# Sliding-window attention, then a gated feed-forward block, on one core: score units of 128 queries shifted by 64 in 64x64 tiles

## The chip, the core and the metric

The kernel runs on one core of one Trainium2 chip. The metric is the device time of one execution in microseconds (us). The kernel before took 308.55 us (median of three runs, 308.38 to 308.95). The profiled execution is one more run of the same kernel, and it took 309.3 us; its trace spans 307.5 us from the first instruction to the last, and 1.8 us lie around the span.

## What is computed

There are 8 batches, 8 heads, 576 tokens and 64 elements a head. A query sees itself and the 127 keys before it, with a bias that falls linearly with distance, by another slope in each head. The attention output is put together to rows of 512 and goes through two matrix products with a gate between them.

```python
B, H, S, D = q.shape                                   # 8, 8, 576, 64
scores = scale * np.matmul(q, k.transpose(0, 1, 3, 2))
rel = pos[:, None] - pos[None, :]
mask = (rel >= 0) & (rel < 128)
scores = np.where(mask, scores - slopes[h] * rel, -1e9)
attn = softmax(scores)                                 # over keys
x = concat_heads(attn @ v)                             # 4608 x 512
h = x @ w_in                                           # 512 x 2048
out = (h * np.cos(h)) @ w_out                          # 2048 x 512, written as f32
```

## The kernel before

**Products of the block.** The 4608 tokens are nine chunks of 512. For a chunk, `moe1` (L758) makes 16 groups of four matmuls (L764, 512 columns each) from the transposed rows `xT`; ScalarE takes the cosine as a sine (L769) and VectorE multiplies (L773) into `gT`. `moe2` (L806) makes 64 matmuls a chunk (L817), whose results ScalarE or VectorE copies out (L824, L825) and a store on the SyncE queue writes to memory (L829). The two halves of a chunk are 128 matmuls of 512 columns.

**Attention units.** `units` (L547) cuts a batch into eight units. The first holds queries 0 to 127 for all heads with 128 key columns a head; six hold 128 queries of four heads with 256 key columns (the block before and the own block); the last holds the last 64 queries for all heads. A unit is 1024 score columns over 128 key partitions. `scores` (L554) makes it with pairs of 64x128 matmuls, one head of a pair in array rows 0 to 63 and the other in 64 to 127 (L573), into two banks of PSUM: `SLOT` gives banks 4 and 5, 6 and 7, 2 and 3 to the units of a visit. `exps` (L596) makes one exponential of 1024 columns (L600); `mask` (L605) multiplies by the exponential of the bias, which is 0 outside the window (L619); `pv` (L622) multiplies by the values, 65 columns a matmul with a column of ones for the sum (L635, L639, L647, L649), 128 wide stationary blocks of the probabilities; `norm` (L662) divides (L672, L675, L684, L686). The rows are then transposed into `xT`: `x_pe` (L693) on TensorE with a copy behind it (L726, L735), or `x_dma` (L740) with a transposing DMA on the SyncE queue (L748, L751).

**Order.** `attention(us, phase)` (L835) takes the units of one phase, of which each chunk has one up to chunk 6 (`QUOTA` units, L342), and makes them in visits of the sizes in `GROUPS` (L338): one call of `scores` for all units of a visit, the exponentials, then for each unit mask, values, norm and transpose. The first four units of a phase go to `xT` by DMA (list `begin`). Then come the loads for later batches: `load_v` on the GpSimd queue, which waits for the DMAs in `begin`, `dma_transposes` (L412) of q and k on the SyncE queue, and `load_nat` (L403) on GpSimd, which waits until those transposes have read the buffer.

All of this only registers operations with a planner (`Plan`, L35). `Plan.schedule` (L95) gives each operation a start from written costs (`occ`, `lat`), takes the lowest priority number first (values 1, scores 2, `moe1` 5, `moe2` 6), and allows one ScalarE function table at a time (phase c exponentials have table 2c+2, the sines of chunk c have table 2c+1). The order on each engine is then fixed: at run time an engine waits for the semaphores of its next instruction and passes over nothing. So `moe2` of chunk c fills TensorE while phase c runs, and `moe1` of chunk c+1 follows.

Of the kernel before, what the change touches and what calls it, by code (L numbers as in the profile page):

```python
# [13 lines left out]
NBLK = 5  # L14
# [273 lines left out]
def bass_alibi_sliding__then__act_gcu_kernel(  # L288
# [8 lines left out]
    with ExitStack() as ctx:  # L297
        def sb(name, shape, dt=BF16):
            return ctx.enter_context(nc.sbuf_tensor(name, shape, dt))
# [17 lines left out]
        NP = 6  # L317
        p_all = sb("p", [128, NP, 1088])
        P = [p_all[:, i, :] for i in range(NP)]
# [13 lines left out]
        off = sb("off", [128, 2, 128], F32)  # L333

        ps = ctx.enter_context(nc.psum_tensor("ps", [128, 8, 512], F32))
# [57 lines left out]
        def load_v(b, order=range(NBLK), behind=()):  # L393
            for t in order:
# [6 lines left out]
                   occ=900, lat=7 * rows)  # L401

        def load_nat(which, src, b):  # L403
            fns = []
            for t in range(NBLK):
                rows = 128 if t < 4 else 64
                fns.append(lambda e, t=t, rows=rows: e.dma_start(  # L407
                    nat[which][0:rows, t, :, :],
                    src[b, :, 128 * t:128 * t + rows, :].rearrange("h p d -> p h d")))
            op("pool", fns, w=[("nat", which)], dma=f"ldn{which}", occ=4400, lat=5500)  # L410
# [29 lines left out]
        def constants():  # L440
# [15 lines left out]
            for i in range(2):  # L456
                op("dve", lambda e, i=i: e.memset(vp[i][:, :, :, 64:65], 1.0), w=[("vinit", i)],
                   pri=5 * i)
                op("dve", lambda e, i=i: e.memset(vp[i][64:128, 4, :, 0:64], 0.0),
                   w=[("vinit", i)], occ=270, pri=5 * i)  # L460
# [7 lines left out]

        def tail_zero(b):
            op("dve", lambda e: e.memset(  # L470
                tr["k"][b % 2][:, :].rearrange("p (c k t) -> p c k t", c=NBLK, k=NPAIR)[
                    :, 4, :, 64:128], 0.0), w=[("tr", "k", b % 2), ("ktail", b % 2)], occ=250,
               lat=300)

# [70 lines left out]


        def units(b):  # L547
            return [(b, 0, 0)] + [(b, qb, hh) for qb in range(1, 4) for hh in range(2)] + [
                (b, 4, 0)]

        def t_first(u):
            return S * u[0] + 128 * u[1]

        def scores(us, slot, after=()):  # L554

            def f(e):
                ins = None
                for n, u in enumerate(us, slot):
                    b, qb, hh = u
                    banks = [SLOT[n], SLOT[n] + 1]  # L560
                    acc = u in BIASED
# [15 lines left out]
            for n, u in enumerate(us, slot):  # L577
                keys += tkeys(u)
                held += [("B", SLOT[n] + x) for x in range(2)]
                occ += 250 if u[1] == 4 else 230  # L580
                if u in BIASED:
                    b, qb, hh = u
                    for x in range(2):
# [6 lines left out]
                           occ=216, lat=379, pri=2, after=after)  # L590
            return op("pe", f, r=keys, w=held, occ=occ, lat=occ + 165, mode=1, pri=2)

        pcount = [0]
        pbuf = {}
# [10 lines left out]
        def mask(u):  # L605
            b, qb, hh = u
            i = pbuf[u]
            if u in BIASED:
                return
            if qb == 0:  # L610
                p = P[i][:, 0:1024].rearrange("p (x k f) -> p x k f", x=2, k=4)
# [4 lines left out]
            else:  # L616
# [3 lines left out]
               r=[("P", i), ("EM", 0), ("EM", 1)], w=[("P", i)], occ=600, lat=690, pri=1)  # L620

        def pv(us):  # L622

            def f(e):
                ins = None
                for u, ub in us:
                    b, qb, hh = u
                    i, V = pbuf[u], vp[b % 2]
                    if qb in (0, 4):
                        for x in range(2):  # L630
# [22 lines left out]
            for u, ub in us:  # L653
                b, qb, hh = u
                wide = qb in (0, 4)
                reads += [("P", pbuf[u]), ("vinit", b % 2)]
                reads += [("v", b % 2, t) for t in range(max(0, qb - 1), qb + 1)]
                held += [("B", x) for x in ([ub, ub + 1] if wide else [ub])]
                occ += 480 if qb == 4 else 240
            op("pe", f, r=reads, w=held, pri=1, occ=occ, lat=occ + 165)  # L660

        def norm(u, ub, n):  # L662
            b, qb, hh = u
            rc = rec[n % 4]
            if qb in (0, 4):
                m = 64 if qb else 128
# [20 lines left out]
                o, U[:, :, :, 0:64], rv[:, :, :, None].broadcast_to([128, 2, 2, 64]), ALU.mult),  # L687
               r=[("rec", n % 4)], w=[("B", ub), key], occ=340, lat=425, pri=0)

        def xkeys(prs, t0, n):  # L690
            return [("xT", pr, t // 64) for pr in prs for t in range(t0, t0 + n, 64)]

        def x_pe(u, ub, n):  # L693
            b, qb, hh = u
            t0 = t_first(u)
            every = range(NPAIR)
            if qb in (0, 4):
                m = 64 if qb else 128
# [40 lines left out]

        def x_dma(u, n):  # L740

            b, qb, hh = u
            t0 = t_first(u)
            if qb in (0, 4):
                m = 64 if qb else 128
                src_, key = (xtl[b % 2], ("xtl", b % 2)) if qb else (xfirst, "xfirst")
                return op(
                    "sp", [lambda e: e.dma_start_transpose(xT[:, :, t0:t0 + m], src_[:, :])],  # L748
                    r=[key], w=xkeys(range(NPAIR), t0, m), dma=f"xt{b % 2}" if qb else "xf",
                    occ=1250, lat=500)  # L750
# [84 lines left out]
        def attention(us, phase):  # L835

            begin, made, g = [], [], 0
            sizes = ([[3, 2, 2]] + GROUPS + [[], []])[phase + 1]
            own = phase >= 0 and 3 in sizes
            for many in sizes:  # L840
# [13 lines left out]
                else:  # L854
                    scores(some, 0)
                    for n, u in enumerate(some):
                        exps(u, n, 2 * phase + 2)
                if not own:
# [6 lines left out]
                else:  # L865
                    sets = [[x] for x in zip(some, SLOT)]
                for set_ in sets:
# [4 lines left out]
                    for u, ub in set_:  # L872
# [4 lines left out]
                        after.append((soon, t_first(u) // CH > phase + 1, u, ub, n))  # L877
                    for soon, late, u, ub, n in after:
                        if soon:
                            begin.append(x_dma(u, n))  # L880
# [37 lines left out]
        for c in range(NCH):  # L918
            if c == 0:
# [63 lines left out]
```

## Time and profile before

| what | value |
|---|---|
| median of three runs | 308.55 us |
| profiled execution | 309.3 us |
| span of its trace | 307.5 us |
| TensorE busy | 302.1 us, 98% |
| ScalarE busy | 199.9 us, 65% |
| VectorE busy | 194.4 us, 63% |
| GpSimd busy | 95.7 us, 31% |
| mean granted TensorE clock | 1.000 |

A row of the instruction groups reads: line, engine, operation, what it writes and reads, shape, count, then busy us and mean ns of one, then the idle time of the engine just before them and what ended it. PE is TensorE, PEld its weight loads, ACT ScalarE, DVE VectorE, POOL GpSimd, SP SyncE; a q behind the name is the engine's queue of DMA issues. A row of the chain of work reads: start in us, length in us, engine, what is written, line and count.

### The profile page before, as it was taken

Reading aid. Unit: us, or ns where it says so; the run is one execution under the profiler, and the core shown is the slowest. Engines: PE = TensorE matmul, PEld = TensorE weight load, DVE = VectorE, ACT = ScalarE, POOL = GpSimd, SP = SyncE. Lnnn points to the kernel's source line nnn. Section 1 sums busy time; section 2 is a strip of 40 time slices with the busy share of each in tenths; the row PEclk is TensorE's granted clock in tenths of the full one; section 3 lists DMA queues with packets and bytes.
Section 4 is the critical chain, followed back from the end, with each engine's and each line's share of the span. In section 5 each row is a group of like instructions: output and inputs, shape, how many; then the busy total and the mean of one; then the engine's idle time right before and its main releaser. Section 6 shows DMA issues by size and latency. Waiting matters only on the chain.

```text
span 307.5 us, 6459 instructions
## 1 busy us (share of the span) xinstructions
PE 302.1 (98%) x2605; PEld 156.5 (51%) x2605; DVE 194.4 (63%) x402; ACT 199.9 (65%) x267; POOL 95.7 (31%) x120
## 2 busy tenths in 40 slices
PE   7899999999999999999999999999999999999996
PEld 5585455445544555445544554455445554444444
DVE  6587667586578566856785568657966588742000
ACT  6897765885487746883688378736964588752211
POOL 8996200555055505550348033900400000000000
PEclk9999999999999999999999999999999999999999
DMA  7999999999699939999699959994991420001112
GB/s 161 179 206 206 207 158 174 167 152 166 125 123 142 175 104 141 131 162 109 157 130 160 151 98 158 153 182 98 154 118 44 113 70 0 0 0 70 68 73 97
DMA packets 149788, 39.08 MB, mean 127 GB/s; under 512 B 138624, under 2 KB 144768, under 8 KB 149760
## 3 DMA queue, kind: packets, MB, share of 16 engines
q0 software_dynamic: 100144, 18.10, 80.1%
q1 hardware_dynamic: 49344, 20.33, 32.8%
q8 instruction: 20, 0.33, 0.4%
q10 hardware_dynamic: 272, 0.26, 0.3%
q14 instruction: 8, 0.07, 0.1%
HBM read 36.70 MB, written 9.44 MB: 150 GB/s over the span
## 4 chain that ended last, share of the span: by engine, by line
PE 88%; DMA 9%; POOL 2%; issue 0%; ACT 0%; POOLq 0%; ACTq 0%
PE ps L817 41%; PE ps L764 36%; DMA w_outb<-in_moe_w_out_dram 7%; PE ps L573 5%; DMA krows<-in_k_dram 2%; PE ps L647 2%; PE ps L649 2%; PE ps L635 1%; PE ps L639 1%; POOL qrows L389 0%; PE ps L726 0%; PE ps L514 0%; PE ps L587 0%; POOL w_inb L428 0%; POOL w_outb L435 0%; POOL krows L389 0%
## 5 line engine op out<-in xcount | busy, mean ns | idle before, releaser
L817 PE MATMUL ps<-w_outb,gT 128*128 128x512 bf16 (+2 forms) x592 | 136.8, 374 | 0.3 <-DMA w_outb<-in_moe_w_out_dram 0.3
L764 PE MATMUL ps<-xT,w_inb 128*128 128x512 bf16 x544 | 122.7, 379 | 0.0
L773 DVE TENSOR_TENSOR gT<-ps,cos 128x512 bf16<-128x512 f32 x136 | 90.6, 688 | 21.3 <-ACT cos L769 16.3
L769 ACT ACTIVATE cos<-ps,halfpi 128x512 f32<-128x512 f32 x136 | 90.1, 688 | 19.3 <-PE ps L764 14.4
L764 PEld LDWEIGHTS ps<-xT,w_inb 128*128 128x128 bf16 x544 | 51.8, 98 | 59.8 <-DVE gT L798 0.7
L817 PEld LDWEIGHTS ps<-w_outb,gT 128*128 128x128 bf16 x592 | 53.3, 98 | 56.5 <-DMA w_outb<-in_moe_w_out_dram 1.2
L600 ACT ACTIVATE p<-ps 128x1024 bf16<-128x1024 f32 x64 | 61.4, 1024 | 31.4 <-PE ps L573 31.2
L396 POOL DMA_DIRECT2D vp<-in_v_dram x40 | 33.8, 866 | 88.2 <-DMA xT<-xnat 65.8
L619 DVE TENSOR_TENSOR p<-p,emask 128x1024 bf16<-128x1024 bf16 x58 | 39.2, 683 | 25.5 <-ACT p L600 25.5
L824 ACT ACTIVATE ob<-ps 128x512 f32<-128x512 f32 (+2 forms) x21 | 12.1, 577 | 42.2 <-PE ps L817 42.1
L407 POOL DMA_DIRECT2D qnat<-in_q_dram x30 | 25.3, 872 | 19.0 <-DMA qt<-qnat 19.0
L407 POOL DMA_DIRECT2D knat<-in_k_dram x30 | 25.3, 876 | 15.1 <-DMA kt<-knat 12.1
L825 DVE COPY ob<-ps 128x512 f32<-128x512 f32 x16 | 10.9, 683 | 16.1 <-PE ps L817 16.1
L686 DVE TENSOR_TENSOR xnat<-ps,rec 128x256 bf16<-128x256 f32 x48 | 19.9, 421 | 1.4
L573 PE MATMUL ps<-qt,kt 64*128 64x128 bf16 (+1 forms) x576 | 19.2, 211 | 0.1
L573 PEld LDWEIGHTS ps<-qt,kt 64*128 64x128 bf16 x576 | 14.5, 94 | 9.6 <-DVE xnat L686 3.4
L647 PEld LDWEIGHTS ps<-vp,p 128*128 128x128 bf16 x192 | 14.2, 97 | 9.2 <-issue 6.4
L647 PE MATMUL ps<-vp,p 128*128 128x65 bf16 x192 | 17.3, 193 | 0.4 <-ACT p L600 0.4
L649 PE MATMUL ps<-vp,p 128*128 128x65 bf16 x192 | 17.3, 193 | 0.0
L649 PEld LDWEIGHTS ps<-vp,p 128*128 128x128 bf16 x192 | 13.1, 97 | 2.3
L684 DVE RECIPROCAL rec<-ps 128x4 f32<-128x4 f32 x48 | 8.2, 176 | 5.2 <-PE ps L649 4.5
L600 ACT ACT_TABLE_LOAD x7 | 9.0, 1283 | 0.1
(63 smaller groups left out, 144.6 us busy)
## 6 DMA issues: line engine op xcount, KB each, us to landing
out_dram<-ob SPq DMA_DIRECT2D x35, 256.0 KB, 2.2
vp<-in_v_dram POOLq DMA_DIRECT2D x32, 128.0 KB, 6.9
qnat<-in_q_dram POOLq DMA_DIRECT2D x24, 128.0 KB, 6.6
knat<-in_k_dram POOLq DMA_DIRECT2D x24, 128.0 KB, 4.9
w_outb<-in_moe_w_out_dram POOLq DMA_DIRECT2D x4, 512.0 KB, 22.3
w_inb<-in_moe_w_in_dram POOLq DMA_DIRECT2D x3, 512.0 KB, 11.4
qrows<-in_q_dram POOLq DMA_DIRECT2D x1, 576.0 KB, 15.1
krows<-in_k_dram POOLq DMA_DIRECT2D x1, 576.0 KB, 18.1
```

Of the source, the lines that this page charges most:

```text
L396: op("pool", [lambda e, t=t, rows=rows: e.dma_start(vp[b % 2][0:rows, t, :, 0:64], v[b, :, 128 * t:128 * t + rows, :].rearrange("h p d -> ...
L407: fns.append(lambda e, t=t, rows=rows: e.dma_start(nat[which][0:rows, t, :, :], src[b, :, 128 * t:128 * t + rows, :].rearrange("h p d -> p ...
L573: ins = e.matmul(ps[:, banks[x], c0:c0 + n_], keys_ap(b, x, pr, kc), query_ap(b, x, pr, qb, n_), start=not acc, stop=stop)
L600: op("act", lambda e: e.activation(P[i][:, 0:1024], ps[:, banks[0]:banks[0] + 2, :].rearrange("p a b -> p (a b)"), ACTF.Exp, scale=0.125), ...
L619: op("dve", lambda e: e.tensor_tensor(p, p, m, ALU.mult), r=[("P", i), ("EM", 0), ("EM", 1)], w=[("P", i)], occ=600, lat=690, pri=1)
L647: e.matmul(o, P[i][:, c0:c0 + 128], V[:, qb - 1, h, 0:65], start=True, stop=False)
L649: ins = e.matmul(o, P[i][:, c0 + 128:c0 + 256], V[:, qb, h, 0:65], start=False, stop=True)
L686: op("dve", lambda e: e.tensor_tensor(o, U[:, :, :, 0:64], rv[:, :, :, None].broadcast_to([128, 2, 2, 64]), ALU.mult), r=[("rec", n % 4)], ...
L764: op("pe", lambda e, kc=kc: e.matmul(ps[:, bank, :], w_in[:, kc, 128 * fc:128 * fc + 128], xT[:, kc, r0:r0 + CH], start=(kc == 0), stop=(k ...
L769: op("act", lambda e: e.activation(cosb[ci][:, :], ps[:, bank, :], ACTF.Sin, bias=halfpi[:, 0:1]), r=["halfpi"], w=[("B", bank), ("cos", c ...
L773: op("dve", lambda e: e.tensor_tensor(gT[gi][:, fc, :], ps[:, bank, :], cosb[ci][:, :], ALU.mult), r=[("cos", ci)], w=[("B", bank)] + [("g ...
L817: op("pe", lambda e, t=t, fc=fc, bank=bank, j0=j0, j1=j1: e.matmul(ps[:, bank, 0:j1 - j0], gT[gi][:, fc, 128 * t:128 * t + 128], w_out[:, ...
```

## The change

Batches 0 and 1 stay as they are. For batches 2 to 7 (`banded`):

- **Units.** Eight equal units, (j, half of the heads), j from 0 to 3. Unit j holds queries 64+128j to 191+128j and needs 192 key columns a head in place of 256: both 64-key halves of block j against all 128 queries, and one 64x64 corner for each half from the neighbouring blocks. Queries 0 to 63 of a batch hang on the two units with j = 0, whose spare corner is used for them.
- **Scores.** 16 matmuls in 64x64 tiles for a unit: eight of 128 columns and eight of 64, in fours over the four tiles.
- **Visits.** `GROUPS` gives phases 2 to 5 two visits of four units in place of 3, 3 and 2. In a visit of four the units lie side by side in banks 2 to 7 (`home`), and one exponential covers 768 columns of two units; values go to banks 2, 5, 4, 7 (`SIDE`), those of queries 0 to 63 to banks 3 and 6. Phase 1 has visits of 4, 3 and 1, and the last unit of batch 1 is moved behind four units of batch 2.
- **Last phase.** The nine units of phase 6 become five in phase 6 (visits of 4 and 1) and four in a new phase 7.
- **Masks.** Two multiplications of 512 elements a unit in place of one of 1024, and a third of 256 for j = 0; the factor tables are made in `band_factors` during chunk 0 (three iotas on GpSimd, some ten VectorE operations, 24 exponentials on ScalarE).
- **Values.** Eight matmuls a unit, and four more for j = 0. Half of them need the values shifted by 64 rows: `copy_v` makes them by three DMAs from SBUF to SBUF on the GpSimd queue behind each `load_v`, which wait for its landing. `tail_zero` is gone.

```diff
-        GROUPS = [[2] * 4] + [[3, 3, 2]] * 5 + [[3] * 3]
+        GROUPS = [[2] * 4, [4, 3, 1]] + [[4, 4]] * 4 + [[4, 1], [4]]
+        SIDE, SIDE_KEY = [2, 5, 4, 7], [3, 3, 6, 6]
-        QUOTA = [8, 8, 8, 8, 8, 8, 9]
+        QUOTA = [8, 8, 8, 8, 8, 8, 5, 4]
...
+        def copy_v(b):
+            V, W = vp[b % 2], vb[b % 2]
+            op("pool", [
+                lambda e: e.dma_start(W[0:64, 0:4, :, :].rearrange("p t h c -> p (t h c)"),
+                                      V[0:64, 1:5, :, :].rearrange("p t h c -> p (t h c)")),
...
+               r=[("v", b % 2, t) for t in range(NBLK)] + [("vinit", b % 2)],
...
+               dma=f"cv{b % 2}", occ=2200, lat=3000)
...
+        def band_factors():
...
+            for h in range(H):
...
+                    op("act", lambda e, o=o, lo=lo, hi=hi, s=slopes[h]: e.activation(
+                        o, bdif[:, lo:hi], ACTF.Exp, scale=s),
+                       r=["bdif"], w=w + ["bem"], occ=180 + (hi - lo) * 5 // 7,
+                       lat=280 + (hi - lo) * 5 // 7, table=2, pri=7)
...
         def units(b):
+            if banded(b):
+                return [(b, j, hh) for j in range(4) for hh in range(2)]
...
+        def band_scores(e, u, n, side):
...
+            for i in range(2):
+                for half in range(2):
+                    for x in range(2):
...
+                        ins = e.matmul(flat[64 * half:64 * half + 64, c0:c0 + 128],
+                                       kt[lo, j, pr, 64 * half:64 * half + 64], two,
+                                       start=True, stop=True)
+            for i in range(2):
+                for half in range(2):
+                    for x in range(2):
...
+                        ins = e.matmul(flat[64 * half:64 * half + 64, c0:c0 + 64], kk, qq,
+                                       start=True, stop=True)
...
+        def exps_side(some, n, table):
...
+            for x in range(2):
+                c0 = home(n, True, x)
+                op("act", lambda e, x=x, c0=c0: e.activation(
+                    p_all[:, i:i + 2, 384 * x:384 * x + 384],
+                    flat[:, c0:c0 + 768].rearrange("p (u f) -> p u f", u=2), ACTF.Exp,
+                    scale=0.125),
...
+                op("dve", lambda e: e.tensor_tensor(p1, p1, own_em[:, gs, :], ALU.mult),
+                   r=[("P", i), "bem"], w=[("P", i)], occ=330, lat=420, pri=1)
+                op("dve", lambda e: e.tensor_tensor(
+                    o, p2[:, :, None, :].broadcast_to([128, 4, 2, 64]),
+                    out_em[0 if qb else 1][:, gs, :].rearrange("p g (y f) -> p g y f", y=2),
+                    ALU.mult), r=[("P", i), "bem"], w=[("P2", i)], occ=330, lat=420, pri=1)
...
+                            e.matmul(o, P[i][:, c0:c0 + 128], V[:, qb, h, 0:65],
+                                     start=True, stop=False)
+                            ins = e.matmul(o, P[i][:, c1:c1 + 128], W[:, qb, h, 0:65],
+                                           start=False, stop=True)
+                        for m in range(4 if qb == 0 else 0):
...
+                            ins = e.matmul(ps[:, kbank[u], 65 * m:65 * m + 65],
+                                           pk[hh][:, c0:c0 + 128], W[:, 0, 4 * hh + m, 0:65],
+                                           start=True, stop=True)
...
+        every.insert(19, every.pop(15))
...
                 load_nat("k", k, 2)
+                band_factors()
...
                 load_v(next_v, behind=begin)
+                copy_v(next_v)
...
-                if next_t < 4:
-                    tail_zero(next_t)
```

More of the change, by code (lines that the diff above doesn't have):

```diff
@@ L578, in scores @@
                 keys += tkeys(u)
[L579 to L580 removed]
+                held += [("B", x) for x in (home_banks(n, side) if banded(u[0]) else
+                                            [SLOT[n], SLOT[n] + 1]) if ("B", x) not in held]
+                occ += 185 if banded(u[0]) else 250 if u[1] == 4 else 230
                 if u in BIASED:
@@ L838, in attention @@
             sizes = ([[3, 2, 2]] + GROUPS + [[], []])[phase + 1]
-            own = phase >= 0 and 3 in sizes
+            own = phase >= 0 and max(sizes + [0]) > 2
             for many in sizes:
@@ L878, in attention @@
                     for soon, late, u, ub, n in after:
+                        if banded(u[0]) and u[1:] == (0, 1):
+                            x = x_dma(u, n, True)
+                            begin += [x] if soon else []
                         if soon:
```

189 lines of the change are left out of this document (166 added, 23 removed).

## The prediction

> **What bounds the kernel now.** I read the page first: its busy times, its slices, then the chain of work that ended last.
>
> ```profile
> PE 302.1 (98%) x2605; PEld 156.5 (51%) x2605; DVE 194.4 (63%) x402; ACT 199.9 (65%) x267; POOL 95.7 (31%) x120
> PE   7899999999999999999999999999999999999996
> PEclk9999999999999999999999999999999999999999
> DMA  7999999999699939999699959994991420001112
> PE 88%; DMA 9%; POOL 2%; issue 0%; ACT 0%; POOLq 0%; ACTq 0%
> ```
>
> PE is busy in every slice but the first two and the last, at full clock; the chain is PE's for 88% of the span, and the DMA's 9% lie in the start. A busy PE can still run below its rate, so the stretches of chunks 3 and 4 come next (us, then busy us of each engine), and the pieces of the chain inside the second.
>
> ```profile
> core 0: us, PE busy (x) PEld busy (x) DVE busy (x) ACT busy (x) POOL busy (x), PEclk, DMA share, GB/s
> 121.50:153.40 31.90, 31.90 (x271) 16.05 (x271) 22.47 (x45) 21.52 (x28) 12.00 (x15) 1.00 1.45 139
> 153.40:184.80 31.40, 31.40 (x269) 15.86 (x268) 21.34 (x43) 22.55 (x30) 12.66 (x17) 1.00 1.48 135
> ```
>
> ```profile
> 165.02 2.16 PE ps L817 x10
> 167.18 0.79 PE ps L573 x32
> 167.96 3.77 PE ps L817 x17
> ...
> 172.44 0.24 PE ps L635 x8
> ...
> 175.30 0.78 PE ps L573 x24
> 176.07 2.05 PE ps L817 x9
> ...
> 180.84 0.55 PE ps L573 x16
> ```
>
> Ten matmuls of `moe2` take 2.16, so 0.216 each. The 128 matmuls of a chunk are then 27.65. Scores are three pieces, 0.79 + 0.78 + 0.55 = 2.12. Values are 72 matmuls a batch at 0.24 / 8 = 0.03, so 2.16. That is 31.9, the whole stretch (its edges cut off a few matmuls of neighbours, either way): nothing waits, and **what is taken from PE is taken from the time**, what is taken from ACT alone is not. What PE must wait for newly is added in full, since its order is fixed.
>
> **The price of score matmuls.** x24 against x16 is eight matmuls, four pairs, for 0.23: 0.0575 a pair of 128 columns. The x16 piece is 8 pairs, 0.46, so entering a visit costs 0.09. The x32 piece holds the unit with 16 matmuls of 64 columns and two others; against x24 it is 0.01 more for 16 of 64 in place of 8 of 128, so a pair of 64 columns costs 0.24 / 8 = 0.03, and one start comes every 0.015. Leaving a visit shows in the next piece: 17 x 0.216 = 3.67 of 3.77, 9 x 0.216 = 1.94 of 2.05, about 0.10. A visit costs about 0.2 beside its matmuls.
>
> **A. Scores, 48 units.** Before: seven units of four pairs and one of eight small pairs a batch, 7 x 0.23 + 0.24 = 1.85, six times 11.1. After: 8 matmuls of 128 and 8 of 64 a unit, in fours over four tiles. No run here shows four tiles at once. The pairs of L573 share the array by rows. The transposes of L514 share it by columns (the weight loads' shapes: 64x128 against 128x64):
>
> ```profile
> 9.94 0.57 PE ps L514 x16
> L573 PEld LDWEIGHTS ps<-qt,kt 64*128 64x128 bf16 x576 | 14.5, 94 | 9.6 <-DVE xnat L686 3.4 <-issue 3.4 <-ACT xT L735 0.8
> L514 PEld LDWEIGHTS ps<-ident,qrows 128*64 128x64 bf16 x64 | 1.8, 110 | 0.5 <-issue 0.4
> ```
>
> Sixteen in 0.57, less 0.09 of entry, are 0.06 a pair of 128 columns: columns overlap as rows do. Both together should let four run in the time of two: a unit is 2 x 0.0575 + 2 x 0.03 = 0.175, 48 are 8.4, so **A = -2.7**. Bounds: four in the time that 64 columns need anywhere would be 4 x 0.03 = 0.12, 5.8 in all, -5.3, which I exclude for the 128 column halves since none in the trace passes below 0.0575; above, a start every 0.015, the tightest in the trace, is 0.24 a unit, +0.4; two at a time is 0.35 a unit, +5.7. I take 0.175, as both kinds of pairs overlap fully.
>
> The column tiles' loads are longer, 110 ns against 94; at 128 columns that is hidden, and at 64 nothing shows it. If the two small groups took a long pair's 0.0575 for it, the unit would be 0.23 and A nothing. The Trainium skill, page "TensorEngine Tiling (Array Packing)", section "Gotcha 2: Feature Incompatibilities", says that column tiling excludes the fast weight load; the longer loads agree, and by it alone A would lie between this nothing and the -2.7.
>
> **B. Visits.** Phases 2 to 5 go from three to two: four visits at 0.2, **-0.8**. Phase 1 keeps three, phases 6 and 7 have three for phase 6's three. One visit of phase 1 mixes old and new tiles: one more change, **+0.1**.
>
> **C. Values and transposes on PE.** Values are 6 x 8 + 2 x 12 = 72 matmuls a batch, as before: **0**. Transposes by `x_pe` behind phase 0 go from 8 matmuls (four units) to 12, by the rule of `soon` and `late`; each with 128 columns at the 0.0575 above: **+0.2**.
>
> **D. ACT and DVE.** They are off the path as long as a phase does not outlast PE's filler.
>
> ```profile
> L600 ACT ACTIVATE p<-ps 128x1024 bf16<-128x1024 f32 x64 | 61.4, 1024 | 31.4 <-PE ps L573 31.2
> L735 ACT ACTIVATE xT<-ps 128x256 bf16<-128x256 bf16 x8 | 3.0, 388 | 7.7 <-PE ps L726 7.7
> L619 DVE TENSOR_TENSOR p<-p,emask 128x1024 bf16<-128x1024 bf16 x58 | 39.2, 683 | 25.5 <-ACT p L600 25.5
> L686 DVE TENSOR_TENSOR xnat<-ps,rec 128x256 bf16<-128x256 f32 x48 | 19.9, 421 | 1.4
> L684 DVE RECIPROCAL rec<-ps 128x4 f32<-128x4 f32 x48 | 8.2, 176 | 5.2 <-PE ps L649 4.5
> L675 DVE TENSOR_TENSOR xfirst<-ps,rec 128x256 bf16<-128x256 f32 x16 | 6.7, 422 | 0.2
> ```
>
> From 1024 and 388 ns an exponential is 0.176 + 0.83 ns an element: 768 cost 0.81, eight a phase 6.5 in place of 8.2, off the path. A mask of 512 elements lies between half of 683, 0.34, and 0.68; I take 0.4, nearest to half. DVE's phase gains 8 x (0.8 - 0.68) + 2 x (0.3 + 0.6), for the third mask and the second division of j = 0, less 2 x 0.42 for the second half that the two wide divisions (L675) lose: +2. One turn from scores to division and back goes with the third visit, by the pieces above 175.30 - 167.18 = 8.1 for a turn of three units, of which about 3 is latency before the first mask. So a phase stays near its 17.6 (167.18 to the end of the stretch, 184.80): **0**. If the masks cost 0.68 each, DVE adds 8 x 0.56 = 4.5 more, and the cover (DVE idles 9 to 10 a stretch) is used up where it matters.
>
> **E. Chunk 0.** The 24 exponentials are 16 x 0.28 + 8 x 0.23 = 6.3 on ACT.
>
> ```profile
> 36.00:54.10 18.10, 18.09 (x213) 9.85 (x214) 11.03 (x30) 10.87 (x15) 0.00 (x0) 1.00 2.00 172
> 30.75 1.56 POOL L407 DMA_DIRECT2D knat<-in_k_dram  x2 [2.99 <-issue]
> ```
>
> POOL is free for the iotas at 32.3, and ACT has 18.1 - 10.9 = 7.2 idle there. A filler of 0.28 can hold back an exponential or a copy on the path; between 0 and one for each of four visits, 1.1; I take **+0.3**, one.
>
> **F. DMAs.** `copy_v` puts a wait at the head of POOL's queue; behind it stand the ten `load_nat` issues.
>
> ```profile
> 150.84 4.19 POOL L396 DMA_DIRECT2D vp<-in_v_dram  x5 [13.03 <-DMA xT<-xnat]
> 159.50 4.19 POOL L407 DMA_DIRECT2D qnat<-in_q_dram  x5 [4.47 <-DMA qt<-qnat]
> 165.18 4.19 POOL L407 DMA_DIRECT2D knat<-in_k_dram  x5 [1.48 <-DMA kt<-knat]
> DMA to landing us min/median/max: 6.6/7.4/10.3
> xT<-xnat SPq DMA_TRANSPOSE x32, 3.2
> 171.57 0.19 PE L635 MATMUL ps<-vp,p 128*128 128x65 bf16 x1
> 176.35 1.25 SPq L751 DMA_TRANSPOSE xT<-xnat  x1
> 179.35 1.17 SPq L751 DMA_TRANSPOSE xT<-xnat  x1
> ```
>
> The last value load is issued at about 154.3 and lands 7.4 to 10.3 later (the row is for the five of this chunk), 161.7 to 164.6. Three issues at 4.19 / 5 = 0.84 end at 164.2 to 167.1; with a landing of 3.2 (the transposes' median) to 7.4 the shifted values stand at 167.4 to 174.5. The first PV of the phase is at 171.57, and needs the old batch; the next ones come 0.3 and more later. All four DMAs that `load_v` waits for now come from the first visit, so I move this 2 earlier, from the step 176.35 to 179.35 less one issue of SP: 165.4 to 172.5 against 171.9. So **0**, with up to +0.6 a phase as the upper end. `load_nat`, issued in 8.4 behind the copies, ends at 170.6 to 173.5 instead of 169.4 and lands by 180.9; the transposes that read it were issued behind the `begin` that ends at 180.5: just covered. Two more function tables are loaded on ACT, beside PE.
>
> **G. The split phase.** Four units now run beside `moe2` of chunk 7, and `moe1` of chunk 8 needs them:
>
> ```profile
> 250.16 22.66 PE ps L764 x105
> 276.71 28.33 PE ps L817 x147
> ```
>
> Before, PE ran through. Now scores, two exponentials, four times mask and division, and a transpose (about 1 + 1.8 + 4 x 1.4 + 3 = 11.4) must fit beside 64 x 0.216 = 13.8 of `moe2` plus 1.8 of own PE work: **0**, at worst +1.5.
>
> **Sum.** -2.7 - 0.8 + 0.1 + 0.2 + 0.3 = -2.9. The profiled execution of 309.3 (span 307.5, 1.8 around it) becomes 306.4; the median of 308.55 becomes **305.7**.
>
> **Rivals.**
> 1. *Starts on PE are the bound.* Fours do not start faster than single matmuls in the trace: 0.015 each, A = +0.4, sum +0.2, 308.8: no change; slow loads in the small groups, A = 0, give 308.4, no change as well. For it: no row shows less than 0.015. Against: both kinds of pairs go at the speed of their columns, so nothing in the trace was held back by starts. If tiles only go by twos, A = +5.7, sum +5.5, 314.1. The Trainium skill, page "TensorE: Matmul & The Clock Gate", section "Wait — 56ns, not 53.3ns?", has a floor of about 25 ns from start to start; by it a unit would be 16 x 0.025 = 0.4, A = +8.1 and the time 316.5. The 16 small matmuls at 0.015 stand below that floor here, so the trace disagrees where two tiles take turns.
> 2. *Shifted values come late* (slower). PE stands at the first value matmul of the new batch with `moe2` queued behind it, while `copy_v` waits for `load_v`. Its place is phases 2 to 6, its price the lateness each time. It decides from 2.9 / 5 = 0.6 a phase: at 1 us, +5, 310.7. For it: the slices with DMA at 9; against: the 2 us of an earlier `begin`.
> 3. *The phase outlasts the filler* (slower). Masks at 0.68 lengthen a phase by 4.5, of which the moved `moe1` hides perhaps 3; six phases at 1 are +6, 311.7.
> 4. *The split phase stalls* PE before chunk 8's `moe1` by up to 1.5: 307.2, still faster.
>
> **How the numbers follow.** Forecast 0.51, its own range 304.4 to 306.8. Rival 4 0.10; rival 1 by starts or loads 0.12, by twos, or by a floor above the 0.015 of the trace, 0.05; rival 2 0.14; rival 3 0.08. A measurement of this kernel tells about 0.2%, 0.6 us, from no change. Faster: 0.51 + 0.10 = 0.61. Same: rival 1 by starts or loads, 0.12. Slower: 0.05 + 0.14 + 0.08 = 0.27. The range goes from 304.4, a unit 0.02 cheaper than taken with nothing lost in E, to 310.7, the middle of rival 2: it leaves out rival 1 by twos, rival 3 and half of rival 2, 0.20.
>
> **What would show it.** Right: a visit of four in a piece of 0.09 + 4 x 0.175 = 0.79 with 64 score matmuls; two such in phases 2 to 5; stretches near 31.2; no idle PE before value matmuls. Wrong: that piece at 1.05 (starts) or 1.5 (twos); PE idle with the DMA of the shifted values as releaser (rival 2); masks of 512 at 0.68 and ACT or DVE in the chain (rival 3); idle PE near 250 to 270 (rival 4).

## The result and the profile after

The changed kernel takes 312.18 us (median of four runs, 311.29 to 313.93) against 308.65 before: a ratio of 1.0113, 95% interval 1.0079 to 1.0146. It is slower, and 1.5 us above the upper end of the predicted range. The profiled execution took 312.87, its span is 311.0. Medians and ratios here leave out executions in a slower state of the chip; with them r1_repeat is 311.8, r3_other_batch 317.74, r6_tiny_copy 309.18, r11_dve_copy_held 316.12 and r12_dve_copy_2 310.86, and some of the expectations go by those figures.

Busy times and slices, on the page of the kernel after:

```profile
PE 301.8 (97%) x2945; PEld 157.7 (51%) x2945; DVE 201.9 (65%) x482; ACT 202.4 (65%) x294; POOL 106.2 (34%) x141
PE   7799999999999999999999999997899999999996
PEclk9799999999999999999999999999999999999999
DMA  7999999999999996999999949999994310130012
```

Two things are new. PE has a hole inside the kernel (7 and 8 in slices 28 and 29), and the DMA engines are full in slices that had room before: of five digits below 9 in slices 2 to 30 before, two are left. The clock row is the granted TensorE clock in tenths. Its dip at the start (digit 7) stands behind a wait of 2.1 for a late q load; the next profile of the same kernel (r1) lacks it.

The score matmuls did nearly what was forecast. Pieces of the chain after, around one visit of four units (start, length, engine, line, count):

```profile
169.78 0.26 PE ps L661 x8
170.03 0.06 PE ps L675 x6
170.10 0.11 PE ps L661 x8
170.21 0.06 PE ps L675 x6
170.27 0.11 PE ps L661 x8
...
170.62 1.40 PE ps L1031 x6
```

One unit is 0.11 + 0.06 = 0.17. The whole visit takes 170.62 - 169.78 = 0.84, 0.05 more than the 0.79 of the forecast, since entering it costs 0.84 - 4 x 0.17 = 0.16 and not 0.09. ScalarE and VectorE as well, by the groups after:

```profile
L735 ACT ACTIVATE p<-ps 128x768 bf16<-128x768 f32 x44 | 34.5, 809 | 17.3 <-PE ps L675 16.7
L773 DVE TENSOR_TENSOR p<-p,qfirst 128x512 bf16<-128x512 bf16 x48 | 18.8, 411 | 9.8 <-ACT p L735 8.8
L675 PEld LDWEIGHTS ps<-qt,kt 64*64 64x64 bf16 x384 | 8.5, 107 | 0.0
```

An exponential of 768 takes 0.81, a mask of 512 takes 0.41. What went wrong stands in the waits after (us in total, times, longest):

```profile
PE ps L978 <- DMA xT<-xtail: 2.6, 1, 2.6
PE ps L583 <- DMA qrows<-in_q_dram: 2.1, 1, 2.1
PE ps L978 <- DMA xT<-xnat: 0.5, 1, 0.5
POOL qrows L424 <- DMA vp<-in_v_dram: 25.9, 3, 10.1
POOL krows L424 <- DMA vp<-in_v_dram: 22.1, 3, 8.3
```

PE waits in front of `moe1` (L978) for rows that `x_dma` transposes, and GpSimd stands 48.0 us in six waits at the head of `copy_v` (L424), 8.0 each. The wait on L583 is the late q load at the start. The link between the other two is in the times from issue to landing, that is, until the data of a DMA has arrived. First come the first visit's transposes of one phase, before and after, then the q and k loads (L438) of that phase after; the last line of each answer is the time from issue to landing.

```profile
L751 SPq DMA_TRANSPOSE xT<-xnat x2: 1244/1692/2139, 207.7 to 210.7; - x2
DMA to landing us min/median/max: 2.4/2.8/3.3
```

```profile
L965 SPq DMA_TRANSPOSE xT<-xnat x4: 1187/1240/1244, 207.8 to 212.9; - x4
DMA to landing us min/median/max: 5.5/7.7/8.5
```

```profile
L438 POOL DMA_DIRECT2D qnat<-in_q_dram x5: 730/897/953, 198.9 to 202.5; - x5
L438 POOL DMA_DIRECT2D knat<-in_k_dram x5: 778/933/952, 203.2 to 206.6; - x5
DMA to landing us min/median/max: 5.6/7.2/7.9
```

The last k load is issued at 206.6, and these loads need 5.6 to 7.9 to land; the transposes that `moe1` waits for are issued from 207.8 on, while the loads are under way, and take 7.7 where they took 2.8. The one that PE waits for longest is that of `xtail`, in the chain:

```profile
211.64 6.63 DMA xT<-xtail
```

A late landing alone is nothing new: in the kernel before, two transposes issued at 127.3 and 128.5 took 6.7 to 7.0, and PE waited for neither. What is new is that it falls on the first visit, whose rows `moe1` needs soon. Even so PE waits in two phases only: 2.6 us here, and 0.5 at about 144, where the transposes took 6.4.

### The profile page after: what moved, and what is told of

Same layout as the page of the kernel before. It is cut to its first block, busy times and chain, and to the rows that moved or that the text cites. A ratio compares the mean times of both kernels' runs of the same rounds, so it can differ in the third digit from the quotient of the medians.

```text
span 311.0 us, 7248 instructions
## 1 busy us (share of the span) xinstructions
PE 301.8 (97%) x2945; PEld 157.7 (51%) x2945; DVE 201.9 (65%) x482; ACT 202.4 (65%) x294; POOL 106.2 (34%) x141
## 4 chain that ended last, share of the span: by engine, by line
PE 88%; DMA 6%; DVE 2%; ACT 1%; SPq 1%; issue 0%; POOL 0%; POOLq 0%; DVEq 0%; ACTq 0%
PE ps L978 38%; PE ps L1031 36%; DMA qrows<-in_q_dram 3%; PE ps L1002 2%; DMA xT<-xtail 2%; PE ps L661 2%; PE ps L583 2%; PE ps L813 2%; PE ps L815 2%; DMA xT<-xnat 1%; PE ps L701 1%; ACT p L757 1%; PE ps L675 1%; PE ps L716 1%; PE ps L939 1%; DVE xnat L887 1%
## 5 line engine op out<-in xcount | busy, mean ns | idle before, releaser
L978 PE MATMUL ps<-xT,w_inb 128*128 128x512 bf16 x544 | 121.0, 379 | 3.1 <-DMA xT<-xtail 2.6
L978 PEld LDWEIGHTS ps<-xT,w_inb 128*128 128x128 bf16 x544 | 51.9, 98 | 63.9 <-DMA xT<-xnat 2.7
L735 ACT ACTIVATE p<-ps 128x768 bf16<-128x768 f32 x44 | 34.5, 809 | 17.3 <-PE ps L675 16.7
L1039 DVE COPY ob<-ps 128x512 f32<-128x512 f32 x13 | 9.0, 691 | 26.9 <-PE ps L1031 26.4
L438 POOL DMA_DIRECT2D knat<-in_k_dram x30 | 25.6, 915 | 1.6 <-issue 1.6
L438 POOL DMA_DIRECT2D qnat<-in_q_dram x30 | 25.8, 891 | 0.0
L773 DVE TENSOR_TENSOR p<-p,qfirst 128x512 bf16<-128x512 bf16 x48 | 18.8, 411 | 9.8 <-ACT p L735 8.8
L887 DVE TENSOR_TENSOR xnat<-ps,rec 128x256 bf16<-128x256 f32 x60 | 24.7, 417 | 0.7
L757 ACT ACTIVATE p<-ps 128x1024 bf16<-128x1024 f32 x16 | 15.7, 1026 | 6.8 <-PE ps L675 4.0
L775 DVE TENSOR_TENSOR p<-p,bias 128x512 bf16<-128x512 bf16 x48 | 18.8, 409 | 0.2
L885 DVE RECIPROCAL rec<-ps 128x4 f32<-128x4 f32 x60 | 10.3, 175 | 13.0 <-PE ps L815 9.5
L813 PEld LDWEIGHTS ps<-vp,p 128*128 128x128 bf16 x192 | 14.8, 97 | 6.9 <-issue 3.2
L813 PE MATMUL ps<-vp,p 128*128 128x65 bf16 x192 | 17.9, 193 | 0.0
L424 POOL DMA_DIRECT2D qrows<-vp x3 | 1.6, 539 | 25.9 <-DMA vp<-in_v_dram 25.9
L661 PE MATMUL ps<-qt,kt 64*64 64x128 bf16 x384 | 10.2, 220 | 0.0
```

What stands on the lines that cost most here:

```text
L438: fns.append(lambda e, t=t, rows=rows: e.dma_start(nat[which][0:rows, t, :, :], src[b, :, 128 * t:128 * t + rows, :].rearrange("h p d -> p ...
L735: op("act", lambda e, x=x, c0=c0: e.activation(p_all[:, i:i + 2, 384 * x:384 * x + 384], flat[:, c0:c0 + 768].rearrange("p (u f) -> p u f" ...
L757: op("act", lambda e: e.activation(P[i][:, 0:1024], ps[:, banks[0]:banks[0] + 2, :].rearrange("p a b -> p (a b)"), ACTF.Exp, scale=0.125), ...
L773: op("dve", lambda e: e.tensor_tensor(p1, p1, own_em[:, gs, :], ALU.mult), r=[("P", i), "bem"], w=[("P", i)], occ=330, lat=420, pri=1)
L775: op("dve", lambda e: e.tensor_tensor(o, p2[:, :, None, :].broadcast_to([128, 4, 2, 64]), out_em[0 if qb else 1][:, gs, :].rearrange("p g ...
L813: e.matmul(o, P[i][:, c0:c0 + 128], V[:, qb, h, 0:65], start=True, stop=False)
```

## The experiments

**Theory.** The loss is the making of the shifted values: the wait of `copy_v` at the head of GpSimd's queue pushes the q and k loads against the first visit's transposes, and the copies' bytes add to the same traffic. **Rivals.** The shifted values themselves come late at PE (rival 2); the phases outlast PE's filler (rival 3); the split of the last phase stalls (rival 4). Times are medians; the kernel before took 308.6 to 308.9 beside all of these runs.

**r1_repeat**: the kernel after, unedited.

> The changed kernel once more, unaltered. If the 2.3 us by which its first scores of phase 1 came later (72.50 against 70.25) belong to the change, its runs stay at 311.3 to 313.9 and the first q rows land near 9.4 in its trace; if they are chance of that execution, the rows land near 6.9 as before and the time is 310 or less. The idle PE before the block products of chunks 3 and 6 (0.6 and 2.8 in the trace) is there again if waits on transposed rows are the cause.

311.35, ratio 1.008 [1.0044, 1.0117]. The first q rows are on time here (PE waits 0.6 for them instead of 2.1) and the time stays above 311, so their lateness was not the cause. PE waits 2.3 + 0.9 = 3.2 for transposed rows before L978 in its profile, and 0.3 for the shifted values. Here the longer hole also cost clock; stretches before and behind it (last three columns: granted clock, DMA share, GB/s):

```profile
210.00:213.90 3.90, 3.89 (x79) 1.96 (x65) 2.02 (x5) 3.17 (x5) 0.00 (x0) 1.00 2.23 144
216.50:219.00 2.50, 2.50 (x14) 1.11 (x13) 1.16 (x4) 0.27 (x1) 2.03 (x3) 0.50 0.66 132
219.00:221.50 2.50, 2.50 (x26) 1.32 (x25) 1.09 (x5) 1.11 (x2) 2.18 (x3) 0.88 1.46 160
```

2.5 us at half clock and 2.5 at 0.88 cost 1.25 + 0.3, about 1.5 on top of the idle time (an estimate).

**r2_no_copy**: nothing is copied, the products use the unshifted values.

```diff
-                        W = vb[b % 2]
+                        W = V
...
-                copy_v(next_v)
```

> The shifted copies of the values are left out (the unshifted values are used in their place, so the output is not the attention's), everything else is as in the changed kernel. Theory: the wait of the copies on the GpSimd queue pushes the loads of q and k into the time in which the rows of the first visit are transposed, which then land 5 to 8 us after issue in place of 2.3, and PE idles 3.4 in all; without them the transposes land after 2.3 to 3, the idle goes, and the time falls by 3 to 3.5 to about 308.5 (306 if the late start was chance). Rival: the start and the new exponential phases themselves cost the time; then it stays above 311.

306.56, ratio 0.9926 [0.9889, 0.9964]. The k loads and the transposes of the same phase, and the slices of PE:

```profile
L438 POOL DMA_DIRECT2D knat<-in_k_dram x5: 732/893/913, 194.5 to 197.9; - x5
```

```profile
L966 SPq DMA_TRANSPOSE xT<-xnat x4: 1175/1240/2030, 204.2 to 209.3; - x4
DMA to landing us min/median/max: 2.3/2.4/3.2
```

```profile
PE   7899999999999999999999999999999999999996
```

The last k load is issued 6.3 ahead of the first transpose (197.9 and 204.2), against 1.2 in the kernel after (206.6 and 207.8), and the transposes land in 2.4. The hole is gone, and the clock is full in every slice. All the rest of the change is worth -2.3; the making of the shifted values costs 311.35 - 306.56 = 4.8 (5.2 in the expectations below). Between the profiled executions (312.25 and 306.56) it is 5.7: of these, 3.2 for rows, 1.5 of clock and 0.3 for the shifted values make 5.0.

**r6_tiny_copy**: as r2, with `copy_v` in its place and waiting as before, but each of its three copies moves one partition of 64. The first of them:

```diff
-                lambda e: e.dma_start(W[0:64, 0:4, :, :].rearrange("p t h c -> p (t h c)"),
+                lambda e: e.dma_start(W[0:1, 0:4, :, :].rearrange("p t h c -> p (t h c)"),
...
```

> As the kernel without copies (unshifted values used, output not the attention's), but the three copies are issued with their wait for the landing of the values, each for one partition alone, some 0.8% of the bytes. If the wait that holds back the loads of q and k is the cost: 309.5 to 312, rows of the first visit landing 5 us and more after issue in chunks 2 and 5. If the bytes are: 306.5 like without copies.

308.98, ratio 1.0003 [0.9983, 1.0023]. The wait alone is worth 2.4. The other 2.4 come with the bytes, and with the products' own wait for the copies, which r6 drops as well (0.3 in r1). Its transposes land in 6.4, between the 2.4 of r2 and the 7.3 of r1:

```profile
L966 SPq DMA_TRANSPOSE xT<-xnat x4: 1174/1241/1244, 205.1 to 210.2; - x4
DMA to landing us min/median/max: 4.3/6.4/6.8
```

**r3_other_batch**: copies of full size, but of the batch before, so without the wait; the products use these copies, so that the shifted half has the wrong batch.

```diff
-            V, W = vp[b % 2], vb[b % 2]
+            V, W = vp[(b + 1) % 2], vb[b % 2]
...
-               r=[("v", b % 2, t) for t in range(NBLK)] + [("vinit", b % 2)],
+               r=[("v", (b + 1) % 2, t) for t in range(NBLK)] + [("vinit", (b + 1) % 2)],
```

> The copies keep their number and size, but read the values of the batch before, which landed a phase ago, so they wait for nothing (the output then uses wrong values in the shifted half). If the wait for the landing is the cost, this falls like the kernel without copies, to about 308.5; if the traffic of the copies, 3.2 MB more on the DMA engines, is the cost, it stays at 311 to 312.

314.66 (two runs, 313.32 and 316.0), ratio 1.0167 [1.0065, 1.0269]: both expectations missed. The copies now run at once, among k's transposes and ahead of the last of them, and the scores wait for those. The first line is the wait, the second the landing of one such transpose in the chain:

```profile
PE ps L661 <- DMA kt<-knat: 5.0, 4, 2.3
161.61 10.71 DMA kt<-knat
```

In r2 the transposes of that line of the kernel (q's and k's) land in 4.6 to 7.6. So the copies cost 8.1 over r2 here without any wait: what they cost depends on what they run ahead of, and the 2.4 between r6 and r1 is no price of the bytes as such.

**r4_act_queue**: the three copies are issued on ScalarE's queue (`op("act", ...)` in place of `op("pool", ...)`, and planned to land in 6 us instead of 3).

> The same copies, issued from ScalarE's queue, where the planner puts them among the sines; GpSimd goes on to the loads of q and k at once. Theory: most of the 3.4 comes back, less the 2 us or so per chunk that ScalarE gives to the issue, hidden behind PE: 308.5 to 309.5. Rival (traffic, or the values arriving late at PE): no better than 311, with PE idle before value matmuls.

343.8, ratio 1.1123 [1.1023, 1.1222], another miss. The planner takes the values to land earlier than they do, and ScalarE, whose order is fixed, stands at the copies with the sines behind it; then the products are late, and PE waits. The first row says "issue" since the profile shows no releaser for this wait; that it is the copies' wait is what r10 tests.

```profile
ACT cos L983 <- issue: 38.4, 5, 9.4
PE ps L978 <- DVE gT L987: 23.9, 5, 6.5
```

These holes cost clock as well: the mean granted clock of this execution is 0.960, so that up to an estimated 0.04 x 342 = 14 us are lost that way.

**r10_act_queue_late**: r4, with the plan told that these values land 7 us later (`late=7000` in `load_v`).

> The kernel of r4_act_queue (the three copies issued from ScalarE's queue), with one edit: the plan is told that the values of batches 2 to 7 land 7 us later, so that the copies stand later in ScalarE's order. Theory (r4 lost its 31.9 us by ScalarE standing in order at the copies until the values landed, with the cosines behind it): the wait is gone, the bytes are still moved, so the time is no_copy's 306.56 plus the 2.6 that r6 and r1 gave for the bytes, 308.5 to 310.5, and ScalarE's idle time before the copies is under 1 us each. Rival (the copies' issue on ScalarE, or their bytes at that time, was the cost): still over 320.

316.22, ratio 1.0254 [1.021, 1.0297]. 27.6 of r4's 32.4 us over r1 are gone, and the clock is full (1.000), so the wait, with the clock that it cost, was the greater part of its cause. But the expectation missed, since ScalarE still stands 9.0 + 4.4 and PE now waits for masks behind it.

```profile
ACT cos L983 <- issue: 9.0, 4, 2.5
ACT L735 <- issue: 4.4, 2, 2.7
PE ps L813 <- DVE p L775: 3.4, 3, 1.9
```

**r5_copy_between**: `copy_v` stays on GpSimd, but between the q and the k load.

```diff
-                copy_v(next_v)
+                late_v.append(next_v)
...
                     load_nat("q", q, next_t)
+                    while late_v:
+                        copy_v(late_v.pop(0))
                     load_nat("k", k, next_t)
```

> The changed kernel with one thing moved: the copies stand on GpSimd's queue between the load of q and the load of k in place of ahead of both, so that the q load goes out while the values land. Theory (the copies cost 5.2, 311.8 against 306.56 without them, since they push the loads of q and k into the next transposes of rows): q is back where it was before the change and k is late by about 2 in place of 5, so most comes back: 307 to 308.5, faster than before the change or level, with no idle PE ahead of block products. Rival (the traffic of the copies is the cost wherever they stand, as the kernel with copies from another batch suggests): 310 to 313, with PE idle before scores or before block products.

308.94, ratio 0.9999 [0.9975, 1.0023], above the 307 to 308.5 of the theory. Of the 4.8, 2.4 come back. Of the 2.4 left, 2.1 in its profile is rival 2, which has this size only here, since the copies land later:

```profile
PE ps L813 <- DMA qrows<-vp: 1.6, 1, 1.6
PE ps L813 <- DMA krows<-vp: 0.5, 1, 0.5
```

**r7_no_copy_332** and **r8_no_copy_nosplit**: r2 with one part of the change undone, the visits of phases 2 to 5 (r7, shown) or the split of the last phase (r8: nine units in phase 6, in visits of 4, 4 and 1).

```diff
-        GROUPS = [[2] * 4, [4, 3, 1]] + [[4, 4]] * 4 + [[4, 1], [4]]
+        GROUPS = [[2] * 4, [4, 3, 1]] + [[3, 3, 2]] * 4 + [[4, 1], [4]]
```

> The kernel without copies with the visits of phases 2 to 5 set back to 3, 3 and 2 units (the small tiles stay; the output is again not the attention's). My sum gave four visits 0.8: 307.4 against 306.56. Rival: the number of visits is nothing, 306.5, or the turn of the longer visit is a cost and it falls.

> The kernel without copies with the last phase in one piece again, nine units in visits of 4, 4 and 1 behind chunk 6 (output not the attention's). My sum gave the split nothing: 306.56 within 0.5. Rival: the split hides something that one long phase does not, then 1 to 2 more; or it costs its own wait before chunk 8, then up to 1.5 less.

310.3, ratio 1.0058 [1.0035, 1.0081], and 306.92, ratio 0.9947 [0.9929, 0.9966]. Visits of four are worth 310.3 - 306.6 = 3.7 with the new units, not 0.8: with three turns a phase, PE waits for masks.

```profile
PE ps L813 <- DVE p L775: 1.9, 3, 0.7
```

These 1.9 and the 0.8 for visits leave 1.0 that I did not locate. The split is worth 0.4 or nothing, as its interval overlaps with r2's. It does not stall: r2, which has it, shows no PE wait above 0.4 but for one of 1.0 at the start.

**r9_engine_copy, r11, r12, r13**: can the shifted values be made for nothing? `W[0:64, 0:4]` and `W[64:128, 1:4]` keep their partitions, so VectorE or ScalarE can copy them; only `W[64:128, 0]` crosses. In r9 the crossing piece is a load of 64 KB from memory, and the plan takes the values to land 7 us later.

```diff
...
+                op(("act", "dve"),
+                   {"act": lambda e, o=o, i=i: e.activation(o, i, ACTF.Copy),
+                    "dve": lambda e, o=o, i=i: e.tensor_copy(o, i)},
+                   r=[("v", b % 2, t) for t in range(s0, s0 + t1 - t0)] + [("vinit", b % 2)],
...
```

> The shifted values of keys 64 to 575 that keep their partitions (W[0:64,0:4] from V[0:64,1:5], W[64:128,1:4] from V[64:128,0:3]) are copied by VectorE or ScalarE instead of by DMA; the one piece that crosses partitions (W[64:128,0]) is loaded from the values in DRAM, 64 KB, with no wait; and the plan is told that the values land 7 us later, so that the copies stand in their engines' order after the landing. Theory (the wait at the head of GpSimd's queue and the copies' traffic are the whole loss): neither is left, two copies of about 1.3 us a phase fall on engines that have 8 to 11 us of 31 to spare, and the time is that of no_copy, 306.56, plus at most 1: 306.2 to 307.6, no PE idle over 0.5 us before a first moe1. Rival (the copies late on VectorE and ScalarE hold the cosines or masks behind them, or come late at the first output products): PE idles 0.5 to 1.5 a phase before L815's or L978's like, 308.5 to 311. Under both the computation is complete.

310.08, ratio 1.0049 [1.0027, 1.0071], so the expectation missed. The copies are short (0.8 and 0.6 on VectorE), but the later landing in the plan moved TensorE's own order: where r2 runs 14 matmuls of `moe2` between the second visit's scores and `moe1`, r9 has 8 left to cover the transposes, and PE waits again.

```profile
208.76 3.13 PE ps L1032 x14
```

```profile
L1036 PE MATMUL ps<-w_outb,gT 128*128 128x512 bf16 x8 | 1.9, 379 | 0.2 <-issue 0.2
```

```profile
PE ps L983 <- DMA xT<-xtail: 1.0, 1, 1.0
```

The first fence is a piece of the chain of r2, the second a group of r9 (stretch 216.8 to 222), the third one of its waits. That wait is 1.0 of the 3.5 by which r9 is above r2. Most of the rest is not located, and the profiled execution, 312.86, is 2.8 above the median.

In r11 both copies are VectorE's; the plan is told of no later landing, but holds them back by 5 us.

> r9_engine_copy with two edits: the plan no longer believes that the values land later (in r9 that moved TensorE's own order, with 85 lines of difference in its order against no_copy), but holds only the two copies back by 5 us after the landing that it plans, and it counts them as 1 ns, so that TensorE's order is that of no_copy line for line; both copies are VectorE's. Theory (r9's 310.08 came from TensorE's changed order, not from the copies or the 64 KB): 306.4 to 307.8, no PE idle over 0.6 us after the first 20 us. Rival (VectorE waits for the landing, or the copies come late for the output products, or the 64 KB DMA delays the loads of q and k and with them the transposes): 308.5 to 311.

316.04, ratio 1.0216 [1.019, 1.0242]. TensorE's order is r2's again, and yet it is worse: the fill of the ones column shared a key with the load, and VectorE stood at it.

```profile
DVE krows L425 <- DMA krows<-in_v_dram: 4.9, 1, 4.9
DVE qrows L425 <- DMA qrows<-in_v_dram: 3.5, 1, 3.5
```

In r12 the ones are filled once, ahead, and the crossing piece is one DMA from SBUF that waits for the first value load only.

> r11_dve_copy_held mended by what its profile showed. There VectorE stood 4.9 and 3.5 us at the two fills of the ones column for the 64 KB load (a dependence of mine, not of the data), with the cosine products behind it; and the 64 KB of 128-byte pieces ran ahead of k's transposes, so that scores waited. Here the ones are filled once, ahead; the piece that crosses partitions is copied by one DMA of 64 rows of 1 KB, which waits for the first value load only; VectorE's two copies (about 0.8 and 0.6) and TensorE's order are those of r11. Theory (GpSimd's wait for the last value load and the copies' traffic are the whole loss): 306.4 to 307.8, under before. Rival (any work for the shifted values between the value loads and the q load still costs, as in r5): 308.5 to 310.

310.83, ratio 1.0026 [0.9989, 1.0064], not to be told from no change. VectorE's copies stood among the cosine products, waited 2.2 + 2.0 there for the value loads, and held up products whose PSUM banks the scores take next:

```profile
PE ps L664 <- DVE gT L991: 3.4, 4, 1.3
```

r13 moves them behind the first scores, ahead of the first mask:

```diff
-                    scores(some, 0, side=side)
+                    sc = scores(some, 0, side=side)
+                    for b in sorted({u[0] for u in some if banded(u[0])} - copied):
+                        engine_copies(b, sc)
```

> r12_dve_copy_2 with VectorE's two copies (0.8 and 0.6) put behind the first scores of the phase and ahead of its first mask, where VectorE waited up to 3.9 us for ScalarE's exp; in r12 they stood among the cosine products, and the scores, which take the PSUM banks that these products release, came 0.8 to 1.5 us late four times. TensorE's order is no_copy's. Theory (each way of making the shifted values costs only where it stands ahead of something that TensorE waits for soon): 306.4 to 307.8, no PE idle over 0.5 us at the phases' first scores. Rival (the copies come late at the first output products or delay the masks, or the small DMA still delays k's transposes): 308.3 to 310.5, with PE idle before L819's like.

**307.01** (306.42 to 308.0), ratio 0.9939 [0.9921, 0.9957]: a kernel that leaves nothing out, faster than both, and 0.45 from r2, which copies nothing. PE has no hole, and the clock digits are all 9. Its waits and transposes:

```profile
PE ps L669 <- DMA kt<-knat: 0.6, 1, 0.6
POOL qrows L425 <- DMA vp<-in_v_dram: 5.6, 3, 3.1
POOL krows L425 <- DMA vp<-in_v_dram: 3.1, 2, 1.9
POOL qnat L446 <- DMA qt<-qnat: 4.6, 4, 1.4
```

```profile
L974 SPq DMA_TRANSPOSE xT<-xnat x4: 1169/1240/2217, 205.7 to 210.8; - x4
DMA to landing us min/median/max: 2.3/2.4/3.4
```

GpSimd still waits 8.7 at its small copy, for the first of the five loads, but the q load behind it waited for q's transposes anyway. The landing of the transposes is back at 2.4.

**r14_no_piece**: r13 without the small DMA, so without the first 64 shifted rows of one half.

> r13 without its small DMA: the first 64 shifted rows of the second half (keys 0 to 63 for the queries of the first tile) stay zero, so that part of the values is left out of the sums. It tells what the DMA of 64 rows and GpSimd's wait for the first value load (1.6 us a phase in r12) are worth. Theory: nothing, within 0.5 of r13, since the load of q behind it waits for the transposes of q anyway. Rival (the DMA is what delays k's transposes): 0.8 to 2 below r13, at no_copy's 306.6.

306.42, ratio 0.9931 [0.9911, 0.995]: 0.6 below r13 with overlapping intervals, between the two expectations. The small DMA costs about that or nothing.

## Why the prediction was wrong, step by step

**A, right.** 0.175 a unit was forecast, 0.17 is measured; four tiles do run in the time of two. Rival 1 is out in all its forms: the longer loads of column tiles (107 ns) are hidden at 64 columns too, as 16 of them fit into these 0.17. The Trainium skill, page "TensorE: Matmul & The Clock Gate", section "Wait — 56ns, not 53.3ns?", says that start to start never falls below about 25 ns; the trace disagrees, with 16 matmuls of a unit in 0.17, 0.011 each, over four tiles.

**B, right in sign, too small.** In the chain it is nearly as priced: two visits of 0.84 a phase against 2.12 before, with A in it. But 3.7 stands against 0.8 where the new units would have been left in three visits, because three turns then outlast the filler (1.9 of it are waits for masks). That is rival 3's mechanism, seen where the change avoids it.

**C and E** have no experiment of their own. All steps but F together come to 306.56 in r2 where 305.7 was forecast, inside the forecast's own range of 304.4 to 306.8; the 0.05 more in a visit of four is a part of the 0.9 between. **D, right**: 0.81 and 0.41 against 0.81 and 0.4, and neither engine bounds a phase of two visits. **G, right**: no stall.

**F failed.** It priced `copy_v` at 0 with the words that `load_nat` "ends at 170.6 to 173.5 instead of 169.4 and lands by 180.9", just covered. I followed the late loads only to their own readers, the transposes of q and k. Which transfers then run beside them was not asked, though the numbers were there: the step has first visit transposes at 176.35 and 179.35, before 180.9. Their like took 7.7 from issue to landing instead of 2.8, and `moe1` waits for them with PE's whole order behind it. The delay was too small as well. F moved the end of the loads by 1.2 to 4.1; against the transposes the last k load came 5.1 later (6.3 ahead of them in r2, 1.2 in the kernel after), although the wait itself, 8.0, lay within the 6.7 to 9.6 that F implies (from 150.84 + 4.19 to 161.7 or 164.6). Priced 0, measured 4.8: 2.4 for the wait, and 2.4 that come with the bytes at this place. The upper end that I gave F, +0.6 a phase, was for another reader, the values at PE, and so was the 310.7 at which the range ended.

**Rival 2** was named as the slower side and is not what happened: its 0.3 in r1 is small, and only r5, where the copies stand later, has 2.1 of it. Its price of 310.7 was near the time by chance.

The half clock was not in the sum at all. In r1 it adds 1.5 behind a hole of 2.3. It does not decide the matter: two of the four executions of the result have a mean clock of 1.000, and they took 311.29 and 311.49, still above 310.7 (those of r1 took 310.33 to 311.35). The same page of the Trainium skill, section "Part 1: The HAM clock gate (the "warmup" mystery)", has the clock halved after an idle window of about 3.4 us that runs freely; the trace agrees on the half (0.50), not on so long an idle time, and the hole of 2.6 in the kernel after was followed by no loss of clock (1.00 from 217.5 to 220).

What stays open: the 1.0 of r7, most of r9's 3.5, and why the landings are late enough for PE to wait in two of the phases only.

## What to carry to other kernels

A wait put at the head of a DMA queue delays every transfer behind it; follow each of them not only to its reader but to the transfers it will then run beside, and ask which engine waits for those. In a kernel whose orders are fixed, a helper step is best put where its engine already waits for something else: the same copies cost 4.3 us among the products (r12 over r2) and 0.45 behind the scores (r13). Ask first whether data has to leave its partitions at all.

## What the runs showed of the hardware that I had not expected

Matmuls of 64x64 over four tiles start every 0.011 us, with weight loads of 107 ns beside them. A DMA transpose that lands in 2.4 us when the last plain load is issued 6.3 us ahead of it (r2) takes 6.4 to 7.7 (medians of four) when that load is issued 2 us ahead or later (r6, r1, after). A hole of 2.3 us in PE's work was followed by 2.5 us at a clock of 0.50 in one execution (r1), and one of 2.6 by no loss in another (after). VectorE copies 64 x 2112 bf16 elements in 0.8 us, ScalarE takes 1.52 for 64 x 1584:

```profile
L433 DVE COPY krows<-vp 64x2112 bf16<-64x2112 bf16 x3 | 2.4, 799 | 0.1
L432 ACT ACTIVATE qrows<-vp 64x1584 bf16<-64x1584 bf16 x2 | 3.0, 1520 | 0.3 <-DVE qrows L433 0.3
```

(Groups of r9; busy us, mean ns, idle before.)
